# Linear attention fused with a squared-ReLU FFN: k's partition maximum on VectorE, product units split and put at fixed half steps, two tiles moved to the raw buffers

## The chip, the cores and the metric

The kernel runs on one core of one Trainium2 chip. Times are device microseconds of that core. The engines are named as in the profile: PE is TensorE's matmul, PEld its weight load, DVE is VectorE, ACT is ScalarE, POOL is GpSimd, SP is SyncE, whose queue issues nearly all DMAs. "L182" is line 182 of the kernel before. In the span of a profiled execution the time runs from the first to the last instruction.

## The reference

Inputs q, k and v have 8 batches, 8 heads, 576 positions and 64 features. q gets a softmax over its features, k a softmax over its positions. The attention output is q_s (k_s^T v), and it goes through a feed-forward network without biases, 512 to 2048 to 512, with a squared ReLU. Everything is float32.

```python
q_s = exp(q - max(q, axis=-1));  q_s /= sum(q_s, axis=-1) + 1e-9
k_s = exp(k - max(k, axis=2));   k_s /= sum(k_s, axis=2) + 1e-9
kv  = einsum('bhsd,bhse->bhde', k_s, v)
x   = einsum('bhsd,bhde->bhse', q_s, kv)      # -> (4608, 512), heads side by side
out = maximum(x @ w_in, 0)**2 @ w_out
```

The maximum of k is over the 576 positions. A tile of k has positions in its 128 partitions (five to each of the first 64, four to each of the others), so that this maximum is first taken over the positions within a partition and then over the partitions.

## The kernel before

**Feed-forward work.** The 4608 tokens are nine blocks of 512: block b is the first 512 tokens of batch b (in the order of the tiles), and block 8 the 64 left over from each batch. A block has 16 steps, one for each 128 hidden features (fc). Each operand is split into a high and a low float32r part, and a product is three matmuls, hi.hi, hi.lo and lo.hi. So `ffn_h` issues 12 matmuls into an `h_ps` (L317 to L319), `activate` makes r, r*r, `g_hi` and `g_lo` of it on ACT and DVE (L323, L329, L330, L332), and `ffn_out` issues 12 matmuls into four accumulators `o_ps` (L349 to L351). `ffn_out` runs two steps behind `ffn_h` (LAG). In block 0 the weights are loaded and split as well (`split_weight`). At the end of a block `store` takes the four accumulators to four tiles and out (L362 to L376).

**Attention.** The heads of a batch are four pairs, each a list of units from `attention(b, pr)`: `k_max` (maximum of k), `q_exp`, `k_exp` (L189 subtracts the maximum, L190 is the exponential), `q_norm`, `kv` (20 matmuls into `kv_ps`, L228, then kvs), `q_t` (the transposed q) and the products with kv (`at_ps`, L294, emptied by a copy on ACT, L296, and an addition on DVE, L297, into `xf`; x_hi on ACT, L302, and x_lo on POOL, L303). The pairs of batches 0 and 1 (`early`, n < 8) go another way: their maximum over partitions is two small PE operations through PSUM (`m_ps`, `mb_ps`), and their q is transposed on PE (`qt_ps`). From batch 2 on, the "steady" pairs take the maximum with one POOL instruction (L182), transpose q in 32x32 blocks on DVE into `tb` (L214), send `tb` to DRAM (`bounce`, L218) and fetch it in four pieces as `qT` (L221), and split it into `qs` with ACT (L269) and POOL (L270).

**Order.** Batch 0's attention comes first. After that the attention of batch b+1 is emitted in the 16 steps of block b. Each step has two places for units, the two half steps, one behind `ffn_h` and the other behind `ffn_out`; before, the list `todo` of 32 units is spread evenly over what is left of the block's half steps, pair by pair. The order of emission is only a rank: a planner simulates the engines with its own costs and lets a later instruction pass an earlier one that it does not believe ready, so that in the trace an at_ps stands between two matmuls of one h_ps. On the chip each engine then takes its instructions strictly in the planned order. `load_pair`, behind `kv`, loads k, q and v two pairs ahead.

**Buffers.** SBUF tiles with one tag share its buffers in turn. The tag `raw` has three (RAWB): raw weights, `xf`, the stores' `o` and the left-over tokens `xs`. The tags `ke`, `qn`, `q_hi` and `q_lo` have one each; `q_lo` serves `tb` and the second `qs`. The PSUM pool `ps_a` has two buffers for all of `kv_ps`, `at_ps`, `m_ps`, `mb_ps` and `qt_ps`.

## Time and profile before

| | |
|---|---|
| median of 3 runs | 947.51 us (944.28 to 949.34) |
| profiled execution | 947.84 us, its span 946.0 us |
| granted TensorE clock, mean | 0.987 |
| busy: PE, PEld | 893.3, 701.6 us |
| busy: DVE, ACT, POOL | 554.1, 402.3, 200.8 us |
| L182, the maximum on POOL | 24 instructions, 20.5 us busy |
| L214, block transpose of q | 24 instructions, 840 ns each |
| L294, products | 96 matmuls |

Busy time is how long an engine worked on instructions; matmuls overlap one another, so a busy PE need not be at its peak, and the distance between the starts of two matmuls tells more. "Idle before" and the waits tell how long an engine stood and which instruction ended this; the name "issue" means that the engine waited for nothing that the profile shows. Idle time of an engine off the critical path costs nothing by itself.

### The profile page before, as it was taken

Reading aid. Unit: us, or ns where it says so; the run is one execution under the profiler, and the core shown is the slowest. Engines: PE = TensorE matmul, PEld = TensorE weight load, DVE = VectorE, ACT = ScalarE, POOL = GpSimd, SP = SyncE. Lnnn points to the kernel's source line nnn. Section 1 sums busy time; section 2 is a strip of 40 time slices with the busy share of each in tenths; the row PEclk is TensorE's granted clock in tenths of the full one; section 3 lists DMA queues with packets and bytes.
Section 4 is the critical chain, followed back from the end, with each engine's and each line's share of the span. In section 5 each row is a group of like instructions: output and inputs, shape, how many; then the busy total and the mean of one; then the engine's idle time right before and its main releaser. Section 6 shows DMA issues by size and latency. Waiting matters only on the chain.

```text
span 946.0 us, 12435 instructions
## 1 busy us (share of the span) xinstructions
PE 893.3 (94%) x4288; PEld 701.6 (74%) x4288; DVE 554.1 (59%) x1007; ACT 402.3 (43%) x779; POOL 200.8 (21%) x167
## 2 busy tenths in 40 slices
PE   5888889899999999999999999999999999999997
PEld 3566667677787788877887788778877888888885
DVE  7998986666566655557665657566655432223221
ACT  3565663444454444344544445444444422222221
POOL 2444530222222222222222222223122200000000
PEclk9999999999999999999999999999999999999999
DMA  8665552322242223222242214212311020001001
GB/s 199 172 196 176 169 159 70 100 63 78 58 112 67 67 68 93 72 68 68 65 114 68 67 54 119 72 56 67 92 43 37 24 67 1 1 1 45 1 0 45
DMA packets 99454, 73.17 MB, mean 77 GB/s; under 512 B 52288, under 2 KB 89152, under 8 KB 99392
## 3 DMA queue, kind: packets, MB, share of 16 engines
q1 hardware_dynamic: 99232, 72.12, 28.2%
q8 instruction: 34, 0.56, 0.2%
q10 hardware_dynamic: 160, 0.26, 0.1%
q14 instruction: 28, 0.23, 0.1%
HBM read 54.00 MB, written 18.35 MB: 76 GB/s over the span
## 4 chain that ended last, share of the span: by engine, by line
PE 56%; DVE 18%; issue 11%; DMA 8%; SPq 4%; ACT 3%; POOL 1%; DVEq 0%; ACTq 0%
PE o_ps L349 9%; PE o_ps L350 9%; PE o_ps L351 9%; PE h_ps L319 9%; PE h_ps L317 9%; PE h_ps L318 8%; DMA qt<-in_q_dram 3%; SPq L221 2%; DMA raw<-in_moe_w_out_dram 2%; DMA raw<-in_moe_w_in_dram 2%; DVE w L134 2%; PE at_ps L294 2%; DVE ke L189 1%; DVE g_lo L332 1%; DVE xf L297 1%
## 5 line engine op out<-in xcount | busy, mean ns | idle before, releaser
L349 PE MATMUL o_ps<-wo_hi,g_hi 128*128 128x512 f32 x576 | 233.0, 405 | 0.2 <-ACT g_hi L330 0.2
L351 PE MATMUL o_ps<-wo_hi,g_lo 128*128 128x512 f32 x576 | 229.3, 401 | 2.5 <-DVE g_lo L332 2.5
L350 PE MATMUL o_ps<-wo_lo,g_hi 128*128 128x512 f32 x576 | 230.3, 400 | 0.6 <-POOL wo_lo L138 0.6
L317 PE MATMUL h_ps<-x_hi,wi_hi 128*128 128x512 f32 x576 | 227.9, 398 | 1.1 <-ACT x_hi L149 0.7
L319 PE MATMUL h_ps<-x_hi,wi_lo 128*128 128x512 f32 x576 | 228.9, 397 | 0.0
L318 PE MATMUL h_ps<-x_lo,wi_hi 128*128 128x512 f32 x576 | 228.0, 396 | 0.2
L332 DVE TENSOR_TENSOR g_lo<-r,g_hi 128x512 fp32r<-128x512 f32 x141 | 110.4, 783 | 103.9 <-ACT g_hi L330 99.6
L329 DVE TENSOR_TENSOR r<-r 128x512 f32<-128x512 f32 x133 | 99.5, 748 | 117.6 <-ACT r L323 117.5
L323 ACT ACTIVATE r<-h_ps 128x512 f32<-128x512 f32 x144 | 85.5, 595 | 122.2 <-PE h_ps L319 119.6
L351 PEld LDWEIGHTS o_ps<-wo_hi,g_lo 128*128 128x128 f32 x576 | 110.2, 191 | 29.7 <-DVE g_lo L332 4.7
L330 ACT CAST g_hi<-r 128x512 fp32r<-128x512 f32 x144 | 89.2, 621 | 100.5 <-PE o_ps L350 82.9
L350 PEld LDWEIGHTS o_ps<-wo_lo,g_hi 128*128 128x128 f32 x576 | 110.2, 191 | 26.0 <-POOL wo_lo L138 1.0
L349 PEld LDWEIGHTS o_ps<-wo_hi,g_hi 128*128 128x128 f32 x576 | 109.7, 191 | 25.3 <-issue 0.8
L317 PEld LDWEIGHTS h_ps<-x_hi,wi_hi 128*128 128x128 f32 x576 | 108.9, 190 | 26.2 <-ACT x_hi L149 1.1
L318 PEld LDWEIGHTS h_ps<-x_lo,wi_hi 128*128 128x128 f32 x576 | 109.0, 189 | 25.3 <-DVE x_lo L150 0.9
L319 PEld LDWEIGHTS h_ps<-x_hi,wi_lo 128*128 128x128 f32 x576 | 108.9, 189 | 25.4 <-POOL wi_lo L138 0.7
L270 POOL TENSOR_TENSOR qs<-qT,qs 64x640 fp32r<-64x640 f32 x48 | 79.8, 1663 | 95.1 <-ACT qs L269 75.8
L303 POOL TENSOR_TENSOR x_lo<-xf,x_hi 128x256 fp32r<-128x256 f32 x48 | 44.7, 935 | 206.5 <-ACT x_hi L302 71.2
L189 DVE TENSOR_TENSOR ke<-kt,mb 128x640 f32<-128x640 f32 x24 | 19.8, 824 | 84.0 <-POOL mb L182 84.0
L190 ACT ACTIVATE ke<-ke 128x640 f32<-128x640 f32 x32 | 23.6, 738 | 104.4 <-DVE ke L189 104.4
L182 POOL PARTITION_ALL_REDUCE mb<-m x24 | 20.5, 856 | 179.3 <-issue 100.6
L269 ACT CAST qs<-qT 64x640 fp32r<-64x640 f32 x48 | 34.8, 726 | 44.9 <-DMA qT<-bounce 43.9
(82 smaller groups left out, 749.2 us busy)
## 6 DMA issues: line engine op xcount, KB each, us to landing
out_dram<-o SPq DMA_DIRECT2D x70, 128.0 KB, 2.4
raw<-in_moe_w_in_dram SPq DMA_DIRECT2D x16, 512.0 KB, 4.4
raw<-in_moe_w_out_dram SPq DMA_DIRECT2D x16, 512.0 KB, 3.3
bounce<-tb SPq DMA_DIRECT2D x24, 320.0 KB, 2.2
qT<-bounce SPq DMA_DIRECT2D x96, 80.0 KB, 2.2
kt<-in_k_dram SPq DMA_DIRECT2D x32, 160.0 KB, 3.0
qt<-in_q_dram SPq DMA_DIRECT2D x32, 160.0 KB, 3.0
vt<-in_v_dram SPq DMA_DIRECT2D x64, 80.0 KB, 2.6
```

The lines of the kernel that those rows point to most:

```text
L270: nc.gpsimd.tensor_tensor(qs[other], qT[own], qs[own].bitcast(F32), op=ALU.subtract)
L303: nc.gpsimd.tensor_tensor(xl, x[:, :, :HIGH], xh.bitcast(F32), op=ALU.subtract)
L317: nc.tensor.matmul(ps, wi_hi[:, cc, sl], xh[:, cc, :], start=(cc == 0), stop=False)
L318: nc.tensor.matmul(ps, wi_hi[:, cc, sl], xl[:, cc, :], start=False, stop=False)
L319: nc.tensor.matmul(ps, wi_lo[:, cc, sl], xh[:, cc, :], start=False, stop=(cc == NCC - 1))
L323: nc.scalar.activation(r, ps, AF.Relu)
L329: nc.vector.tensor_tensor(r, r, r, op=ALU.mult)
L330: nc.scalar.copy(g_hi, r)
L332: e.tensor_tensor(g_lo, r, g_hi.bitcast(F32), op=ALU.subtract)
L349: nc.tensor.matmul(acc[t], g_hi[:, ts], wo_hi[:, fc, :], start=(n == 0), stop=False)
L350: nc.tensor.matmul(acc[t], g_hi[:, ts], wo_lo[:, fc, :], start=False, stop=False)
L351: prev = nc.tensor.matmul(acc[t], g_lo[:, ts], wo_hi[:, fc, :], start=False, stop=(n == NFC - 1))
```

## The change

1. In steady pairs the maximum over partitions is taken on DVE: `m` (128 partitions by 2 x 64 features) is transposed in 32x32 blocks into `mt`, reduced along the free axis to `m1` (128x4, one partial maximum for each group of 32 partitions and each feature), brought to 32 partitions by four copies (`m4`), reduced over the groups into all four partition groups by four reductions (`m5`), broadcast and transposed back into `mb`. The POOL instruction goes.
2. `k_max` of a steady pair works in a tile of the `raw` tag (`two`), and `ke` is taken only in `k_exp`.
3. `tb` takes a `raw` buffer in place of `q_lo`.
4. `attn` is one product of one head's q and not two: a steady pair has four product units where it had two.
5. `todo` is replaced by `slots`: each unit has a half step of its own. In block 0 pair pr of batch 1 is based at 6 + 6 pr; after that the pairs are 7 half steps apart, from 32 (b - 1) + 1. Offsets follow the order of the units, so a steady pair has k_max at -8, q_exp at -7, q_norm at -5, k_exp at -3, q_t at -1, kv at 0 and the products at 2, 3, 4 and 5. The first pair of batch 2 starts within block 0.
6. `mb` and `left` have one buffer in place of two.

```diff
+FIRST_KV, EARLY_STEP, EARLY_AT = 6, 6, (-6, -5, -3, -2, 0, 1, 2, 3)
+STEADY_STEP, STEADY_AT = 7, (-8, -7, -3, -5, 0, -1, 2, 3, 4, 5)
...
         ps_pool = ps_first if b == 0 and odd else ps_a
 
         def k_max():
-            ke = attn_pool.tile([P, 2, LOW, D], F32, name="ke", tag="q_hi" if odd else "ke", bufs=1)
-            st["ke"] = ke
+            if early:
+                ke = attn_pool.tile([P, 2, LOW, D], F32, name="ke", tag="q_hi" if odd else "ke", bufs=1)
+                st["ke"] = ke
+            else:
+                ke = w_pool.tile([P, 2, 3, D], F32, name="two", tag="raw", bufs=RAWB)
             two, one = ke[:, :, 0:2, :], ke[:, :, 2, :]
             nc.vector.tensor_tensor(two, kk[:, :, 0:2, :], kk[:, :, 2:4, :], op=ALU.max)
             nc.vector.tensor_tensor(one, two[:, :, 0, :], two[:, :, 1, :], op=ALU.max)
...
                 mb = ps_pool.tile([P, 2, 1, D], F32, name="mb_ps", tag="a")
                 nc.tensor.matmul(mb.rearrange("p h o d -> p (h o d)"), mc.broadcast_to([P, P]), ident, start=True, stop=True)
             else:
-                mb = attn_pool.tile([P, 2, 1, D], F32, name="mb")
-                nc.gpsimd.partition_all_reduce(
-                    mb.rearrange("p h o d -> p (h o d)"), m.rearrange("p h d -> p (h d)"), P, bass_isa.ReduceOp.max
-                )
+                mt = attn_pool.tile([P, 4, BLK], F32, name="mt", bufs=1)
+                nc.vector.transpose(mt, m.rearrange("p h (e a) -> p (h e) a", a=BLK))
+                m1 = attn_pool.tile([P, 4], F32, name="m1", bufs=1)
+                nc.vector.tensor_reduce(m1, mt, axis=AX.X, op=ALU.max)
+                m4 = attn_pool.tile([BLK, 4, 4], F32, name="m4", bufs=1)
+                for g in range(4):
+                    nc.vector.tensor_copy(m4[:, g], m1[g * BLK : (g + 1) * BLK])
+                m5 = attn_pool.tile([P, 4, 1], F32, name="m5", bufs=1)
+                for g in range(4):
+                    nc.vector.tensor_reduce(
+                        m5[g * BLK : (g + 1) * BLK, :, 0], m4.rearrange("p g c -> p c g"), axis=AX.X, op=ALU.max
+                    )
+                mb = attn_pool.tile([P, 2, 1, D], F32, name="mb", bufs=1)
+                nc.vector.tensor_copy(mt, m5.broadcast_to([P, 4, BLK]))
+                nc.vector.transpose(mb.rearrange("p h o (e a) -> p (h o e) a", a=BLK), mt)
             st["mb"] = mb
 
         def k_exp():
+            if not early:
+                st["ke"] = attn_pool.tile([P, 2, LOW, D], F32, name="ke", bufs=1)
             ke = st["ke"]
             nc.vector.tensor_tensor(ke, kk, st["mb"].broadcast_to([P, 2, LOW, D]), op=ALU.subtract)
             nc.scalar.activation(ke, ke, AF.Exp)
...
             if early:
                 return
 
-            tb = attn_pool.tile([P, 4, LOW, BLK], F32, name="tb", tag="q_lo", bufs=1)
+            tb = w_pool.tile([P, 4, LOW, BLK], F32, name="tb", tag="raw", bufs=RAWB)
             nc.vector.transpose(
                 tb.rearrange("p c j a -> p j c a"), qn.rearrange("p j h (e a) -> p j (h e) a", a=BLK)
             )
...
                     xh, xl = x_hi[b % 2][:, pr, c0:c1], x_lo[b % 2][:, pr, c0:c1]
                     split(xh, xl, ps)
                 else:
-                    left = attn_pool.tile([P, LEFT], F32, name="left")
+                    left = attn_pool.tile([P, LEFT], F32, name="left", bufs=1)
                     nc.scalar.copy(left, ps)
                     nc.sync.dma_start(x_left[:, pr, b * LEFT : (b + 1) * LEFT], left)
             return go
 
-        def attn(g0, nj):
+        def attn(g0, nj, h):
             def go():
-                N = 2 * nj * BLK
-                xf = w_pool.tile([P, 2, 2, nj, BLK], F32, name="xf", tag="raw", bufs=RAWB)
+                if h == 0:
+                    st[g0] = w_pool.tile([P, 2, 2, nj, BLK], F32, name="xf", tag="raw", bufs=RAWB)
+                xf = st[g0]
                 x, corr = xf[:, 0], xf[:, 1]
-                for h in range(2):
-                    ps = ps_pool.tile([P, 2, nj, BLK], F32, name="at_ps", tag="a")
-                    qs = st["q"][h][:, g0 : g0 + 2, :nj].rearrange("p g j a -> p g (j a)")
-                    nc.tensor.matmul(ps.rearrange("p g j a -> p g (j a)"), kvs[:, h], qs, start=True, stop=True)
-
-                    nc.scalar.copy(corr[half[0]] if h == 0 else corr[half[1]], ps[HALF:])
-                    nc.vector.tensor_tensor(x[half[h]], ps[:HALF], corr[half[h]], op=ALU.add)
+                ps = ps_pool.tile([P, 2, nj, BLK], F32, name="at_ps", tag="a")
+                qs = st["q"][h][:, g0 : g0 + 2, :nj].rearrange("p g j a -> p g (j a)")
+                nc.tensor.matmul(ps.rearrange("p g j a -> p g (j a)"), kvs[:, h], qs, start=True, stop=True)
+
+                nc.scalar.copy(corr[half[h]], ps[HALF:])
+                nc.vector.tensor_tensor(x[half[h]], ps[:HALF], corr[half[h]], op=ALU.add)
+                if h == 0:
+                    return
                 xh, xl = (
                     t[b % 2][:, pr].rearrange("p (j g a) -> p g j a", g=4, a=BLK)[:, g0 : g0 + 2]
                     for t in (x_hi, x_lo)
...
                     nc.sync.dma_start(dst, x[:, :, HIGH])
             return go
 
+        units = [k_max, q_exp, k_exp, q_norm, kv, q_t]
         if early:
-            return [k_max, q_exp, k_exp, q_norm, kv, q_t, attn_early(0, NT), attn_early(NT, S)]
-        return [k_max, q_exp, k_exp, q_norm, kv, q_t, attn(0, LOW), attn(2, HIGH)]
+            return units + [attn_early(0, NT), attn_early(NT, S)]
+        return units + [attn(0, LOW, 0), attn(0, LOW, 1), attn(2, HIGH, 0), attn(2, HIGH, 1)]
 
 
     def h_part(ps, blk, fc, cc):
...
     order0 = list(range(2, PRE)) + list(range(min(2, PRE))) + list(range(PRE, NFC))
     steps = [(0, fc) for fc in order0] + [(blk, fc) for blk in range(1, B + 1) for fc in range(NFC)]
     LAG = 2
-    gs, accs, todo = {}, {}, []
+    gs, accs = {}, {}
+
+    slots = {}
+    for b in range(1, B):
+        for pr in range(NPAIR):
+            if b == 1:
+                base, offs = FIRST_KV + EARLY_STEP * pr, EARLY_AT
+            else:
+                base, offs = 2 * NFC * (b - 1) + 1 + STEADY_STEP * pr, STEADY_AT
+            us = attention(b, pr)
+            nxt = b * NPAIR + pr + NB
+            if nxt < B * NPAIR:
+                us[4] = lambda f=us[4], nxt=nxt: (f(), load_pair(nxt // NPAIR, nxt % NPAIR))
+            for u, o in zip(us, offs):
+                slots.setdefault(base + o, []).append(u)
+    for cc, u in enumerate(left_units()):
+        slots.setdefault(2 * NFC * (B - 1) + 4 + 6 * cc, []).append(u)
     for n in range(len(steps) + LAG):
         if n < len(steps):
             blk, fc = steps[n]
-            if n % NFC == 0:
-                for u in todo:
-                    u()
-                todo = []
-                if blk + 1 < B:
-                    for pr in range(NPAIR):
-                        nxt = (blk + 1) * NPAIR + pr + 2
-                        us = attention(blk + 1, pr)
-                        if nxt < B * NPAIR:
-                            us[4] = lambda f=us[4], nxt=nxt: (f(), load_pair(nxt // NPAIR, nxt % NPAIR))
-                        todo += us
-                elif blk + 1 == B:
-                    todo = left_units()
             if n < PRE:
                 gs[n] = activate(hs[fc], blk, fc)
             else:
...
             for pr in range(NB):
                 load_pair(1, pr)
         m = n - LAG
-        count = -(-len(todo) // max(1, NFC - (2 if blk else 0) - n % NFC)) if n < len(steps) else 0
-        for u in todo[: (count + 1) // 2]:
+        for u in slots.get(2 * n, []):
             u()
-        todo = todo[(count + 1) // 2 :]
         if m >= 0:
             b2, f2 = steps[m]
             if m % NFC == 0:
                 accs[b2] = [ps_o.tile([P, DM], F32, name=f"o_ps{t}", tag="o") for t in range(4)]
             ffn_out(b2, f2, gs.pop(m), accs[b2], m % NFC)
-        for u in todo[: count // 2]:
+        for u in slots.get(2 * n + 1, []):
             u()
-        todo = todo[count // 2 :]
 
 
 # ---- launch: one core; inputs and outputs as the reference has them ----
```

## The prediction, made before the result was known

> **What bounds the kernel now.** I read the page's busy times first, then the span cut at the first output matmul of each token block, then the waits, then two stalls in the timeline.

> ```profile
> span 946.0 us, 12435 instructions
> PE 893.3 (94%) x4288; PEld 701.6 (74%) x4288; DVE 554.1 (59%) x1007; ACT 402.3 (43%) x779; POOL 200.8 (21%) x167
> ```

> TensorE (PE) carries the time; no other engine is busy for two thirds of it. The next view gives, per stretch, its length, then busy time and instructions of PE, weight loads, DVE, ACT and POOL, then the granted clock. The rows are block 0 with the attention of batch 1, blocks 1 to 6 together, each with the attention of the batch after it, block 4 alone as one of these six, and block 7, which has no attention.

> ```profile
> 54.00:174.25 120.25, 109.26 (x505) 83.30 (x506) 105.01 (x173) 69.08 (x128) 41.26 (x27) 0.94 0.52 150
> 174.25:770.42 596.17, 577.19 (x2850) 457.60 (x2849) 356.55 (x659) 265.77 (x531) 140.50 (x118) 0.99 0.26 69
> 475.45:573.65 98.20, 96.22 (x482) 76.35 (x481) 60.78 (x114) 45.32 (x91) 24.04 (x20) 1.00 0.28 74
> 770.42:859.73 89.31, 89.31 (x386) 72.11 (x384) 24.66 (x36) 21.52 (x36) 0.00 (x0) 1.00 0.07 18
> ```

> Block 7 shows the floor: 384 matmuls in 89.31 us with PE never idle, 0.23 us from one start to the next. A block with attention adds 16 product matmuls (at_ps, line 294) and four groups of 20 small ones (kv_ps, line 228). What these must cost is read where nothing waits:

> ```profile
> 537.46 0.39 PE L319 MATMUL h_ps<-x_hi,wi_lo 128*128 128x512 f32 x1
> 537.78 0.80 PE L228 MATMUL kv_ps<-vt,ke 128*64 128x65 f32 x20
> 538.51 0.50 PE L349 MATMUL o_ps<-wo_hi,g_hi 128*128 128x512 f32 x1
> ...
> 545.09 0.39 PE L350 MATMUL o_ps<-wo_lo,g_hi 128*128 128x512 f32 x1
> 545.32 0.46 PE L294 MATMUL at_ps<-qs,kvs 128*128 128x320 f32 x2
> 545.61 0.39 PE L351 MATMUL o_ps<-wo_hi,g_lo 128*128 128x512 f32 x1
> ```

> A kv group adds 538.51 - 537.46 - 0.23 = 0.82 us, two products add 545.61 - 545.09 - 0.23 = 0.29 us. A block with attention therefore needs 89.31 + 4 x 0.82 + 8 x 0.29 = 94.9 us. Six need 569.4, less 0.8 for one kv group that falls outside this stretch: 568.6. They took 596.17. The difference, 27.6 us, is PE waiting, and it is all that a change of the steady attention can win there. The waits name its source:

> ```profile
> ACT ke L190 <- DVE ke L189: 104.4, 27, 7.0
> POOL mb L182 <- issue: 100.6, 17, 6.1
> DVE ke L189 <- POOL mb L182: 84.0, 19, 5.7
> PE at_ps L294 <- DVE xf L297: 13.5, 13, 2.1
> ```

> Before the partition maximum POOL stands 5.9 us (100.6 / 17) waiting for nothing that the trace shows. DVE, which takes its instructions in order, then stands 4.4 us (84.0 / 19) at the subtraction of that maximum, and ACT at the exponential behind it. PE's own longest entry is at_ps, behind the DVE addition (xf) that empties the product's PSUM buffer. One case, engine by engine:

> ```profile
> 514.00 3.21 POOL L270 TENSOR_TENSOR qs<-qT,qs 64x640 fp32r<-64x640 f32 x2 [4.08 <-ACT qs L269]
> 516.47 1.29 DVE L329 TENSOR_TENSOR r<-r 128x512 f32<-128x512 f32 x1
> 518.61 0.28 DVE L171 TENSOR_TENSOR m<-ke,kt 128x128 f32<-128x128 f32 x1
> 523.81 0.82 DVE L189 TENSOR_TENSOR ke<-kt,mb 128x640 f32<-128x640 f32 x1 [4.05 <-POOL mb L182]
> 524.55 0.68 DVE L332 TENSOR_TENSOR g_lo<-r,g_hi 128x512 fp32r<-128x512 f32 x1
> 525.29 0.50 PE L351 MATMUL o_ps<-wo_hi,g_lo 128*128 128x512 f32 x1 [0.16 <-DVE g_lo L332]
> 525.62 0.39 PE L349 MATMUL o_ps<-wo_hi,g_hi 128*128 128x512 f32 x1
> 526.53 0.99 DVE L297 TENSOR_TENSOR xf<-at_ps,xf 64x320 f32<-64x320 f32 x2
> 527.06 0.39 PE L294 MATMUL at_ps<-qs,kvs 128*128 128x256 f32 x1 [1.05 <-DVE xf L297]
> ```

> The maximum m within partitions is ready at 518.9, and its use starts 4.9 us later; g_lo and both xf stand behind it. PE, whose lead is used up by then, waits for g_lo at 525.29 and starts the product at 527.06, 1.44 after the matmul before it instead of 0.23: 1.2 us lost. A second kind of stall has no POOL in it: two product units at each other's heels, four matmuls through two PSUM buffers. Its rows, with the later release of xf by POOL:

> ```profile
> 302.57 0.39 PE L318 MATMUL h_ps<-x_lo,wi_hi 128*128 128x512 f32 x1
> 302.59 0.87 ACT L296 COPY xf<-at_ps 64x320 f32<-64x320 f32 x2
> 303.21 0.99 DVE L297 TENSOR_TENSOR xf<-at_ps,xf 64x320 f32<-64x320 f32 x2
> 303.74 0.39 PE L294 MATMUL at_ps<-qs,kvs 128*128 128x256 f32 x1 [0.78 <-DVE xf L297]
> 307.54 0.74 POOL L303 TENSOR_TENSOR x_lo<-xf,x_hi 128x256 fp32r<-128x256 f32 x1 [7.14 <-ACT xf L296]
> ```

> Here PE loses 303.74 - 302.57 - 0.23 = 0.9 us.

> **The change part by part.** *The all-reduce leaves POOL:* 24 instructions, POOL's stand before them and with it the 84.0 us of DVE. *In its place* DVE gets, per pair, a block transpose of 128x128, a reduction of it to 128x4, four copies and four reductions on 32 partitions each, a broadcasting copy and a second transpose. The nearest rows:

> ```profile
> L214 DVE STREAM_TRANSPOSE tb<-qn 128x640 f32<-128x640 f32 x24 | 20.2, 840 | 3.3 <-PE at_ps L294 2.4 <-PE qt_ps L255 0.9
> L177 DVE TENSOR_REDUCE mc<-m_ps 128x1 f32<-128x128 f32 x8 | 2.2, 274 | 0.3 <-PE m_ps L175 0.3
> L231 DVE RECIPROCAL rs<-rs 128x1 f32<-128x1 f32 x32 | 4.9, 152 | 0.1
> ```

> A 128x128 transpose lies between a fifth of line 214's (0.17 us) and all of it (0.84). I take 0.29, nearer the fifth, since it has a fifth of the elements and even one element takes 0.15. The reduction is line 177's 0.27. The eight small ones lie between 0.07 each, if they overlap as far as half, and 0.27; I take line 231's 0.15. The broadcasting copy lies between 0.15 and the 0.28 of m above, taken as 0.25. Sum: 2 x 0.29 + 0.27 + 8 x 0.15 + 0.25 = 2.3 us, with ends of 1.3 and 4.4; for 24 pairs 55 us, 31 to 106. For a block that is 9.2 us on a DVE busy for 61 of 98, which also loses 84.0 / 6 = 14 us of standing, so it hides under PE's matmuls; were DVE full, it would cost the 9.2. Next in line is ACT's exponential of ke, as now.

> *The four product units* issue the same 16 matmuls, copies, additions and stores per block, but one product per half step (94.9 / 32 = 3.0 us) where a unit had two. A PSUM buffer then has two half steps, 6 us, to be emptied by a copy of 0.4 and an addition of 0.5 (half of the 0.87 and 0.99 above). The planner still reorders, so the half steps are ranks and not times.

> *Raw buffers:* tb no longer waits for the last reader of q_lo (3.3 us in all at line 214, the most that this can win), but two, tb and xf now rotate with the stores through three buffers. At a late buffer DVE would stand with r and g_lo behind it, and PE's line 351 behind those. I take nothing, since the holders are short, and price the loss below. mb goes from two buffers to one, and DVE alone writes and reads it, in order; left too, whose uses in batch 1 lie six half steps apart.

> *Early attention in block 0* now overlaps its pairs and ends four half steps sooner. But mb_ps keeps one of two PSUM buffers for three half steps in which kv_ps, qt_ps and at_ps of the pair before want both, and the first pair of batch 2 adds its k and q chains there. PE idles 120.25 - 109.26 = 11.0 us in this block. A shorter tail may win 6 of them; three waits more, one for each overlapped pair, as long as the longest of at_ps (2.1) may lose 6. I take the middle, nothing.

> *Sum.* Of the 27.6 us I leave 1.5 per block, 9 in all, for starts of kv groups, late kvs or qs and the clock of 0.99. The gain is 18.6. The profiled run took 947.84 us, 1.84 around its span of 946.0; 947.84 - 18.6 = 929.2. The median of the runs, 947.51, is that run's time but for 0.3. I predict 929.

> **The rivals.** *A. Only POOL's part pays.* If the planner bunches products as before, stalls like the 0.9 us at 303.74 stay. One or two a block are 1.4 us; with the 1.5 above, 6 x 2.9 = 17 of 27.6 remain, and the time is 947.8 - 10.2 = 938. For it speaks the planner's freedom, against it the 6 us that a single product has.

> *B. POOL holds up the new chain.* r took 1.29 us at 516.47 (g_lo, of the same shape, 0.68), inside POOL's subtractions from 514.00 to 517.21, and the first maximum of k has a longest of 1730 ns against a median of 415:

> ```profile
> L168 DVE TENSOR_TENSOR ke<-kt x32: 407/415/1730, 4.5 to 713.2; 128x256 f32<-128x256 f32 x32
> ```

> The next pair's k_max now has the half step of q_t, which issues these subtractions. If its operations are held for all 3.2 us, the chain takes 5.5 us. Four of them are 22 us in a block with 37 idle, so DVE does not become the bound; but if at half the pairs xf then comes a microsecond late for PE, 12 us go back, less the fifth or so that spacing absorbs: 939. [...]

> *C. Transposed q comes late: no change.* From q_norm to q_t there are four half steps, 12 us. Transpose, landing of the bounce, four issues and their landing need 0.84 + 2.2 + 1.96 + 2.2 = 7.2. A bounce that stands 10.3 us in SP's queue overshoots by 5.5:

> ```profile
> SPq L101 <- DVE g_lo L332: 81.4, 14, 10.3
> 510.05 1.96 SPq L221 DMA_DIRECT2D qT<-bounce  x4
> bounce<-tb SPq DMA_DIRECT2D x24, 320.0 KB, 2.2
> qT<-bounce SPq DMA_DIRECT2D x96, 80.0 KB, 2.2
> ```

> Three such pairs in the whole run take 16.5 of the 18.6 back: 946. Against it: those queue waits end with DVE work that POOL had held up.

> *D. Slower: the raw ring.* Claims per block rise from 12 (8 xf, 4 stores) to 20. When all three buffers are held by tb and xf, DVE stands for what is left of tb's 3.0 us (0.84 and 2.2), and PE with it. It decides from 1 us of PE per pair, 24 against the gain of 18.6 and the 4.7 below; at the likely 1.3 us the time is 947.8 - 18.6 + 31 = 960. Against it: xf is held for 5.7 us (302.59 to 308.28), so a pair's holds are about 1 + 3.0 + 2 x 5.7 = 15 us, with stores like tb some 74 a block, of 285 that three buffers have.

> **How the numbers follow.** Forecast 0.58, with 917 to 938 as its own range (all of the 27.6 and a little of block 0, or half); A 0.13, B 0.11, C 0.09, D 0.09. About 0.5%, 4.7 us, is what a measurement of this kernel can tell from no change. Faster: 0.58 + 0.13 + 0.11 = 0.82; same 0.09; slower 0.09. The range of 916 to 946 reaches to C and leaves out D and part of C.

> **What would show it.** In the profile after: no line 182 on POOL, no DVE wait for mb, a chain of 2.3 us per pair, blocks 1 to 6 near 96.4 us, PE's wait at at_ps for xf under 4 us. It is wrong if these blocks stay above 98; B shows as stretched maxima and copies, C as at_ps or ACT's qs waiting, D as DVE or ACT standing at a raw buffer. A block 0 that is longer than 120 would show that my nothing there was mis-sized.

## The result and the profile after

The changed kernel takes 916.96 us (median of 4 runs, 915.52 to 917.42) against 946.37 (944.28 to 949.34): a ratio of 0.9684, 95% interval 0.9654 to 0.9715. That is 29.4 us faster; 18.6 had been forecast, as 929 within 916 to 946. The profiled run took 915.52 us with a span of 913.4. The head of its page:

```profile
span 913.4 us, 12612 instructions
PE 879.6 (96%) x4288; PEld 698.0 (76%) x4288; DVE 612.4 (67%) x1295; ACT 400.2 (44%) x779; POOL 178.6 (20%) x143
```

288 instructions were added on DVE and 24 removed on POOL. PE still has its 4288 matmuls. The span, cut again at the first output matmul of each block, in the columns of the prediction (length, then busy time and instructions of PE, weight loads, DVE, ACT and POOL, then the clock): all ahead of block 0's first output matmul, block 0, blocks 1 to 6, block 4 alone.

```profile
0.00:51.90 51.90, 34.88 (x202) 22.06 (x202) 46.77 (x113) 26.70 (x53) 19.11 (x22) 1.00 0.82 203
51.90:167.45 115.55, 105.76 (x496) 79.50 (x497) 110.00 (x191) 66.57 (x125) 39.78 (x28) 0.97 0.52 152
167.45:737.88 570.43, 569.26 (x2860) 459.15 (x2859) 409.20 (x925) 265.63 (x534) 119.73 (x94) 1.00 0.28 73
454.33:549.05 94.72, 94.72 (x483) 76.70 (x481) 71.32 (x162) 44.98 (x90) 20.60 (x16) 1.00 0.29 78
```

Blocks 1 to 6 fell from 596.17 to 570.43, 1.8 above the floor of 568.6 that the prediction had worked out; block 4 runs without a gap on PE. The other 6.8 us of the span's 32.6 were won ahead of block 1: block 0 from 120.25 to 115.55, and 54.0 to 51.9 ahead of it. The marks do not cut off the same work, though: ten matmuls of block 1's h_ps ran in block 0 before and run behind the mark now (2850 recorded in blocks 1 to 6 before, 2860 here). At 0.23 us each that is 2.3 us, so that like for like blocks 1 to 6 won 28.0 and block 0 2.4. DVE no longer waits for mb. The waits after that answer to those shown of before:

```profile
POOL x_lo L326 <- ACT x_hi L325: 355.5, 34, 21.9
ACT ke L211 <- DVE rs L252: 28.4, 13, 5.1
ACT ke L211 <- DVE ke L210: 23.4, 10, 4.7
ACT xf L317 <- DMA out_dram<-o: 11.1, 4, 3.6
PE at_ps L315 <- ACT kvs L267: 1.0, 1, 1.0
```

POOL now simply waits for work. ACT's idle time before the exponential of ke went from 104.4 us to 52.4; only 23.4 of these are now put down to DVE's ke. PE's largest entry for the at_ps of steady pairs (L315) is a single one of 1.0 us, and none names xf. The new DVE instructions, by line (count, then busy time and mean in ns):

```profile
L190 DVE STREAM_TRANSPOSE mt<-m 128x128 f32<-128x128 f32 x24 | 7.3, 305 | 0.4
L192 DVE TENSOR_REDUCE m<-mt 128x4 f32<-128x128 f32 x24 | 6.7, 280 | 0.5
L195 DVE COPY m<-m 32x4 f32<-32x4 f32 x96 | 16.4, 171 | 1.6
L198 DVE TENSOR_REDUCE m<-m 32x4 f32<-32x16 f32 x96 | 16.3, 170 | 1.6
L202 DVE COPY mt<-m 128x128 f32<-128x128 f32 x24 | 9.9, 413 | 0.4
L203 DVE STREAM_TRANSPOSE mb<-mt 128x128 f32<-128x128 f32 x24 | 7.4, 309 | 0.5
```

m1, m4 and m5 all appear as "m". A chain has 305 + 280 + 4 x 171 + 4 x 170 + 413 + 309 = 2671 ns of DVE time, against the 2.3 us put down for it.

### The profile page after: what moved, and what is told of

It reads as the page before. It is cut to its first block, busy times and chain, and to the rows that moved or that the text cites. A ratio compares the mean times of both kernels' runs of the same rounds, so it can differ in the third digit from the quotient of the medians.

```text
span 913.4 us, 12612 instructions
## 1 busy us (share of the span) xinstructions
PE 879.6 (96%) x4288; PEld 698.0 (76%) x4288; DVE 612.4 (67%) x1295; ACT 400.2 (44%) x779; POOL 178.6 (20%) x143
## 4 chain that ended last, share of the span: by engine, by line
PE 80%; DVE 12%; DMA 3%; issue 2%; SPq 1%; ACT 1%; POOL 0%; DVEq 0%; ACTq 0%
PE o_ps L373 13%; PE o_ps L374 13%; PE o_ps L375 13%; PE h_ps L341 13%; PE h_ps L343 13%; PE h_ps L342 12%; DMA raw<-in_moe_w_in_dram 2%; DVE w L137 2%; DVE raw L136 2%; PE kv_ps L249 2%; PE at_ps L315 1%; DVE raw L135 1%; DVE g_lo L356 1%; DMA raw<-in_moe_w_out_dram 1%; DVE ke L210 1%
## 5 line engine op out<-in xcount | busy, mean ns | idle before, releaser
L373 PE MATMUL o_ps<-wo_hi,g_hi 128*128 128x512 f32 x576 | 227.7, 400 | 1.7 <-ACT wo_hi L139 1.1
L353 DVE TENSOR_TENSOR r<-r 128x512 f32<-128x512 f32 x133 | 97.2, 731 | 114.3 <-ACT r L347 113.3
L326 POOL TENSOR_TENSOR x_lo<-xf,x_hi 128x256 fp32r<-128x256 f32 x48 | 42.1, 877 | 356.6 <-ACT x_hi L325 355.5
L291 POOL TENSOR_TENSOR qs<-qT,qs 64x640 fp32r<-64x640 f32 x48 | 81.1, 1689 | 109.2 <-ACT qs L290 97.8
L317 ACT COPY xf<-at_ps 64x320 f32<-64x320 f32 (+1 forms) x96 | 38.0, 396 | 31.1 <-PE at_ps L315 16.2
L318 DVE TENSOR_TENSOR xf<-at_ps,xf 64x320 f32<-64x320 f32 (+1 forms) x96 | 42.5, 443 | 8.5 <-ACT xf L317 6.9
L211 ACT ACTIVATE ke<-ke 128x640 f32<-128x640 f32 x32 | 23.6, 739 | 52.4 <-DVE rs L252 28.4
```

The source lines that it names most:

```text
L291: nc.gpsimd.tensor_tensor(qs[other], qT[own], qs[own].bitcast(F32), op=ALU.subtract)
L318: nc.vector.tensor_tensor(x[half[h]], ps[:HALF], corr[half[h]], op=ALU.add)
L353: nc.vector.tensor_tensor(r, r, r, op=ALU.mult)
L373: nc.tensor.matmul(acc[t], g_hi[:, ts], wo_hi[:, fc, :], start=(n == 0), stop=False)
```

## The experiments

Each ran in several rounds beside the kernel before. "Blocks 1 to 6" is the stretch from block 1's first output matmul to block 7's; as the planner takes more or fewer of block 1's h_ps matmuls ahead of the first of these marks, the matmuls recorded in the stretch (0.23 us each) and the start of block 7 stand beside it. The tail from there is 175.5 to 175.9 us in every kernel.

| kernel | median us | ratio to before, 95% | blocks 1 to 6 | matmuls in it | block 7 starts at |
|---|---|---|---|---|---|
| before | 946 to 949 | | 596.2 | 2850 | 770.4 |
| changed | 916.96 | 0.965 to 0.972 | 570.4 | 2860 | 737.9 |
| e1: before, maximum on DVE | 916.90 | 0.964 to 0.970 | 566.5 | 2851 | 739.7 |
| e2: changed, maximum on POOL | 996.34 | 1.046 to 1.056 | 654.5 | 2862 | 823.5 |
| e3: changed, two products a unit | 918.65 | 0.966 to 0.972 | 572.5 | 2861 | 741.0 |
| e4: changed, early units as before | 920.54 | 0.968 to 0.974 | 565.9 | 2849 | 742.5 |
| e5: before, POOL runs maxima only | 917.27 | 0.967 to 0.972 | 565.8 | 2850 | 739.2 |
| e6: changed, k_max two half steps later | 914.88 | 0.964 to 0.969 | 569.8 | 2862 | 737.4 |
| e7: changed, chain twice | 947.94 | 0.996 to 1.002 | 597.7 | 2863 | 767.5 |
| e8: changed, two raw buffers | 922.53 | 0.972 to 0.979 | 567.4 | 2836 | 745.5 |
| e9: e7 with k_max as in e6 | 943.58 | 0.994 to 0.997 | 600.5 | 2862 | 768.8 |
| e10: e6, block 0 relieved on DVE | 917.84 | 0.965 to 0.971 | 570.6 | 2861 | 741.4 |
| e11: e1 with the chain twice | 935.10 | 0.984 to 0.989 | 585.1 | 2851 | 757.5 |
| e12: e7, qs's low half on DVE | 922.19 | 0.970 to 0.976 | 577.2 | 2862 | 745.4 |

**e1: the maximum alone.** The `else` branch of `k_max` in the kernel before is replaced by the new chain; units, places, `tb` and `ke` stay as they were.

```diff
-                mb = attn_pool.tile([P, 2, 1, D], F32, name="mb")
-                nc.gpsimd.partition_all_reduce(
-                    mb.rearrange("p h o d -> p (h o d)"), m.rearrange("p h d -> p (h d)"), P, bass_isa.ReduceOp.max
-                )
+                mt = attn_pool.tile([P, 4, BLK], F32, name="mt", bufs=1)
+                nc.vector.transpose(mt, m.rearrange("p h (e a) -> p (h e) a", a=BLK))
...
+                nc.vector.transpose(mb.rearrange("p h o (e a) -> p (h o e) a", a=BLK), mt)
...
-                    left = attn_pool.tile([P, LEFT], F32, name="left")
+                    left = attn_pool.tile([P, LEFT], F32, name="left", bufs=1)
```

> The kernel before with the partition maximum on DVE and nothing else of the change (mb and left with one buffer each, which the new small tiles need for their room). Stretch of blocks 1 to 6: 596.2 us before, 570.4 after the whole change, floor 568.6. Theory (POOL's stand makes the larger part of PE's waiting, two products in one unit the rest, about 1.4 us a block): 578 to 582 and a total of 929 to 933. Rival 1 (spacing alone, because a product with 6 us can wait out POOL's stand): over 590, total over 941. Rival 2 (POOL's stand is all): 572, total 919 to 924.

```profile
173.18:739.71 566.53, 566.32 (x2851) 457.66 (x2849) 413.10 (x938) 267.33 (x532) 116.42 (x95) 1.00 0.28 73
```

916.90 us: the whole gain, with two products in a unit, units dealt out from the list and `tb` in q_lo. In 566.53 us of blocks 1 to 6 PE is not busy for 0.2. The theory of two sources of waiting falls, and rival 2, that POOL's stand is all of it, holds, with a little more than it had promised. The stall at 303.74 that the prediction took for a second kind has POOL's stand just ahead of it in the kernel before:

```profile
299.68 0.72 POOL L182 PARTITION_ALL_REDUCE mb<-m  x1 [5.88 <-issue]
300.43 0.83 DVE L189 TENSOR_TENSOR ke<-kt,mb 128x640 f32<-128x640 f32 x1 [5.50 <-POOL mb L182]
```

DVE came out of 5.50 us of standing at 300.43. ACT's part of r had ended at 294.53, yet DVE took r only behind that ke, at 301.18; r, g_lo and the additions that PE waited for had queued there and followed until 304.20. So the bunched products had cost PE time because DVE, behind POOL's stand, came late to empty them.

**e2: the converse.** All of the change but the maximum, which is POOL's again.

```diff
-                mt = attn_pool.tile([P, 4, BLK], F32, name="mt", bufs=1)
...
+                mb = attn_pool.tile([P, 2, 1, D], F32, name="mb")
+                nc.gpsimd.partition_all_reduce(
+                    mb.rearrange("p h o d -> p (h o d)"), m.rearrange("p h d -> p (h d)"), P, bass_isa.ReduceOp.max
+                )
```

> The changed kernel with the maximum given back to POOL's all-reduce in steady pairs; split products, half steps and raw buffers stay. Theory: DVE again stands some 4 us per pair, single products outlast most of it, g_lo does not: 2 us a block come back, blocks 1 to 6 at 580 to 585, total 927 to 932. Rival 1 (spacing alone): 572, total 917 to 919. Rival 2 (POOL's stand is all): over 590, total over 937.

996.34 us: rival 2 had said over 937, but not this much; with the maximum on POOL the new order is slower than the old one by 5%. Blocks 1 to 6, the waits, then POOL's timeline around an all-reduce, with ACT's casts of qs:

```profile
168.93:823.47 654.54, 598.68 (x2862) 477.33 (x2860) 352.64 (x657) 262.78 (x530) 133.11 (x116) 0.95 0.24 62
POOL x_lo L315 <- issue: 84.7, 12, 7.5
POOL qs L280 <- issue: 28.6, 4, 7.5
PE at_ps L304 <- POOL qs L280: 22.9, 6, 4.6
PE h_ps L331 <- POOL x_lo L315: 16.8, 5, 4.2
```

```profile
472.06 0.73 POOL L315 TENSOR_TENSOR x_lo<-xf,x_hi 128x256 fp32r<-128x256 f32 x1 [7.30 <-issue]
478.04 1.48 ACT L279 CAST qs<-qT 64x640 fp32r<-64x640 f32 x2 [1.42 <-DMA qT<-bounce]
478.78 0.72 POOL L190 PARTITION_ALL_REDUCE mb<-m  x1 [5.99 <-ACT qs L279]
487.04 0.71 POOL L315 TENSOR_TENSOR x_lo<-xf,x_hi 128x256 fp32r<-128x256 f32 x1 [7.53 <-issue]
487.83 3.16 POOL L280 TENSOR_TENSOR qs<-qT,qs 64x640 fp32r<-64x640 f32 x2
```

POOL stands not only before the all-reduce but also 7.1 us (84.7 / 12) before the x_lo that follows one, and the same before qs. Here the all-reduce at 478.78 comes ahead of an x_lo and of the subtractions for qs, so both stands delay what PE needs next: ACT's casts of qs ended at 479.5, and POOL began to subtract at 487.83. PE's granted clock fell too, to 0.95 from 0.99 in these blocks; 0.05 of 654.5 us is some 33 us, an estimate, so the waits are not the whole price. In the kernel before, too, x_lo had 42.9 us of such stands in 6 places, but nobody waited for it soon.

**e3: two products a unit**, in the changed kernel.

```diff
-STEADY_STEP, STEADY_AT = 7, (-8, -7, -3, -5, 0, -1, 2, 3, 4, 5)
+STEADY_STEP, STEADY_AT = 7, (-8, -7, -3, -5, 0, -1, 2, 4)
...
-        return units + [attn(0, LOW, 0), attn(0, LOW, 1), attn(2, HIGH, 0), attn(2, HIGH, 1)]
+        return units + [lambda: (attn(0, LOW, 0)(), attn(0, LOW, 1)()), lambda: (attn(2, HIGH, 0)(), attn(2, HIGH, 1)())]
```

> The changed kernel with two products in a unit again, the units at half steps 2 and 4 behind kv. Theory: one or two stalls of 0.9 us per block come back, blocks 1 to 6 at 576 to 580, total 922 to 927. Rival 1 (spacing is what counts): over 585, total over 931. Rival 2 (POOL's stand is all): 570 to 572, total 917.

918.65 us, 1.7 above the changed kernel but from another set of runs, blocks 1 to 6 at 572.5: the split is worth about 2 us at most. This and e1 agree.

**e4: early units as before**, in the changed kernel.

```diff
-FIRST_KV, EARLY_STEP, EARLY_AT = 6, 6, (-6, -5, -3, -2, 0, 1, 2, 3)
+FIRST_KV, EARLY_STEP, EARLY_AT = 4, 8, (-4, -3, -2, -1, 0, 1, 2, 3)
```

> The changed kernel with batch 1's units in block 0 at the half steps that they had before (8 per pair, one after the other, up to the last half step). The change won 2.1 us ahead of block 0's first output matmul and 4.7 us in block 0 (120.3 to 115.6). Theory that the overlap of early pairs won this: block 0 goes back to 119 to 121 and the total to 921 to 924. Rival (it came from elsewhere, the freed q_lo, POOL or the planner's order): block 0 stays within 1 us of 115.6, total 916 to 918.

```profile
53.66:176.59 122.93, 110.50 (x506) 84.80 (x507) 110.64 (x198) 69.28 (x129) 40.27 (x27) 0.93 0.52 152
```

920.54 us, 3.6 above the changed kernel. The two come from different sets of runs and the intervals of their ratios overlap, but block 7 starts 4.6 us later in the trace, so the overlapped early pairs seem to win some 4 us within the new order. Block 0 takes 122.9, with ten matmuls more ahead of the mark (x506 for x496), and its clock is 0.93 where the changed kernel has 0.97. The clock alone could make 5.1 us (0.07 x 122.9 - 0.03 x 115.6, an estimate); whether the early pairs won by fewer waits or by the clock is not shown. But e1 has the old early order and reaches block 7 2.8 us before e4, so the early places are not where the change as a whole won; they make up for what the rest of the new order costs there.

**e5: what POOL's stand is.** The kernel before, its maximum on POOL; the two other steady jobs of POOL go to DVE.

```diff
-                    nc.gpsimd.tensor_tensor(qs[other], qT[own], qs[own].bitcast(F32), op=ALU.subtract)
+                    nc.vector.tensor_tensor(qs[other], qT[own], qs[own].bitcast(F32), op=ALU.subtract)
...
-                nc.gpsimd.tensor_tensor(xl, x[:, :, :HIGH], xh.bitcast(F32), op=ALU.subtract)
+                nc.vector.tensor_tensor(xl, x[:, :, :HIGH], xh.bitcast(F32), op=ALU.subtract)
```

> The kernel before, its maximum still on POOL, with POOL's two other steady jobs (the low half of qs, L270, and x_lo, L303) on DVE, so that from batch 2 on POOL runs all-reduces and nothing else. Theory after the first four runs: POOL's stand of 5.9 us before an all-reduce, and of 7.3 us before the next x_lo, is a change of POOL's program from one kind of instruction to the other, not a price of the all-reduce. Then the stand before mb goes almost wholly, blocks 1 to 6 take 566 to 573 us (596.2 before), total 916 to 923, although DVE gets some 10 us a block more. Rival (every all-reduce pays its 5.9 us): DVE goes on standing 4 us per pair, blocks 1 to 6 at 588 to 600, total 938 to 950.

First the instructions of the maximum in the kernel before, where the second row counts the entries named MODIFY_POOL_CONFIG in POOL's queue at that line, then the same rows here:

```profile
L182 POOL PARTITION_ALL_REDUCE mb<-m x24: 722/722/3330, 138.5 to 720.7; - x24
L182 POOLq MODIFY_POOL_CONFIG  x46: 1/6/21, 125.3 to 714.8; - x46
```

```profile
L182 POOL PARTITION_ALL_REDUCE mb<-m x24: 702/734/3330, 136.9 to 684.4; - x24
L182 POOLq MODIFY_POOL_CONFIG  x2: 8/8/8, 125.3 to 125.3; - x2
...
POOL mb L182 <- DVE m L171: 401.3, 19, 28.5
DVE ke L189 <- POOL mb L182: 0.9, 2, 0.6
```

917.27 us with the maximum still on POOL. Of the 46 entries two are left, both at 125.3, POOL's waits before the maximum are all put down to DVE and none to "issue", an all-reduce takes 0.73 us (median), and DVE's stand has gone from 84.0 us to 0.9. So the stand was not the price of a partition maximum but of POOL going back and forth between two kinds of instruction, some 6 us one way (5.9 in the kernel before) and 7 the other (7.1 in e2). What POOL does in that time no trace shows.

**e6: k_max two half steps later**, in the changed kernel.

```diff
-STEADY_STEP, STEADY_AT = 7, (-8, -7, -3, -5, 0, -1, 2, 3, 4, 5)
+STEADY_STEP, STEADY_AT = 7, (-6, -7, -3, -5, 0, -1, 2, 3, 4, 5)
```

> The changed kernel with a steady pair's k_max two half steps later (offset -6 for -8), so that it no longer has the half step of the pair before's q_t and its POOL subtractions. In the changed kernel the first, second and third maximum have longest times of 1508, 1644 and 1668 ns, the small copies 728, the broadcasting copy 1400. Theory (POOL's subtractions hold these up, and PE does not notice): the mean of the three maxima and of the broadcasting copy falls by a third or more, total stays within 2 us of 917. Rival (holding up the chain costs PE time): total falls by 2 us or more. Other rival (k_max two half steps later makes k_exp late): total over 920.

In the changed kernel, durations by line (least, median and longest ns):

```profile
L175 DVE TENSOR_TENSOR two<-two x24: 223/274/1644, 127.7 to 672.0; 128x128 f32<-128x128 f32 x24
L195 DVE COPY m<-m x96: 150/158/728, 137.5 to 677.4; 32x4 f32<-32x4 f32 x96
L198 DVE TENSOR_REDUCE m<-m x96: 156/171/177, 141.5 to 678.1; 32x4 f32<-32x16 f32 x96
L202 DVE COPY mt<-m x24: 183/226/1400, 144.8 to 678.4; 128x128 f32<-128x128 f32 x24
```

The broadcasting copy fell from a mean of 413 to 280 ns, but the third maximum stayed at 688 (691 in the changed kernel) and the second went from 497 to 453, as if the planner pulled these forward whatever their rank. The expected third was not reached, and the run does not tell apart what it was for. 914.88 us (914.55 to 915.55) is the lowest time of all, 2.1 us under the changed kernel, but from another set of runs, and the intervals of the two ratios overlap.

**e7: the chain twice**, to see what hides it.

```diff
+                for _ in range(2):
+                    nc.vector.transpose(mt, m.rearrange("p h (e a) -> p (h e) a", a=BLK))
...
+                    nc.vector.transpose(mb.rearrange("p h o (e a) -> p (h o e) a", a=BLK), mt)
```

> The changed kernel with DVE's twelve new instructions of each steady pair run twice, with the same result. One pass takes 305 + 280 + 4 x 171 + 4 x 170 + 413 + 309 = 2671 ns of DVE time, so a block has 10.7 us more on a DVE that is busy for 71 of 94.7. Theory (the chain lies under PE's matmuls): blocks 1 to 6 stay at 570 to 573, total 916 to 919. Rival (DVE is close to being the bound, or the chain is on the way of the products): 10 to 60 us more, total 927 to 977.

947.94 us: 27 us more in blocks 1 to 6, and the gain is gone. Blocks 1 to 6, PE's largest entry for at_ps (L316 here), the groups of the second and third maximum, then POOL and DVE around one kv and the product that PE wanted:

```profile
169.81:767.52 597.71, 577.63 (x2863) 462.31 (x2861) 471.49 (x1205) 265.27 (x536) 124.47 (x94) 0.99 0.27 70
PE at_ps L316 <- DVE kvs L153: 15.8, 7, 3.6
L175 DVE TENSOR_TENSOR two<-two 128x128 f32<-128x128 f32 x24 | 12.7, 527 | 0.0
L177 DVE TENSOR_TENSOR m<-two,kt 128x128 f32<-128x128 f32 x24 | 20.5, 854 | 0.4
```

```profile
502.22 3.75 POOL L292 TENSOR_TENSOR qs<-qT,qs 64x640 fp32r<-64x640 f32 x2 [2.75 <-ACT qs L291]
502.56 1.36 DVE L175 TENSOR_TENSOR two<-two 128x128 f32<-128x128 f32 x1
504.45 1.67 DVE L177 TENSOR_TENSOR m<-two,kt 128x128 f32<-128x128 f32 x1
514.61 0.46 DVE L153 TENSOR_TENSOR kvs<-kf,kvs 64x64 fp32r<-64x64 f32 x2
514.96 0.39 PE L316 MATMUL at_ps<-qs,kvs 128*128 128x320 f32 x1 [3.35 <-DVE kvs L153]
```

DVE is busy for 79% of these blocks (471.5 of 597.7 us), yet from 496.3 to 515.1 us no gap on it exceeds 0.05 us: x's additions, the next pair's q and k work, the chain and kvs fall together around this kv. The planned order of PE has the product earlier than that: PE stands 3.35 us at it, and so in seven places, 15.8 us in all.

**e8: two raw buffers**, in the changed kernel.

```diff
-RAWB = 3
+RAWB = 2
```

> The changed kernel with two raw buffers for three. It prices rival D of the prediction, which had holds of some 74 us a block: of 190 buffer microseconds that is two fifths. Theory (the ring has slack in blocks 1 to 6, but weights in block 0 need it): blocks 1 to 6 within 4 us of 570.4, block 0 and the start longer by 3 to 10, total 922 to 931. Rival (the ring is tight, and three buffers just suffice): blocks 1 to 6 longer by 15 us or more, total over 935.

```profile
54.10:178.05 123.95, 113.54 (x520) 83.56 (x521) 111.98 (x197) 69.35 (x130) 40.58 (x28) 0.97 0.50 148
178.05:745.48 567.43, 565.04 (x2836) 454.43 (x2835) 424.08 (x918) 262.80 (x530) 121.27 (x94) 1.00 0.27 72
```

922.53 us. Here 24 matmuls more than in the changed kernel lie ahead of block 1's mark (x520 for x496 in block 0), some 5.5 us. Like for like, blocks 1 to 6 lose 2.5 us with two buffers (567.43 + 5.5 - 570.43), block 0, where weights pass through the ring, 2.9, and the start 2.2. Rival D of the prediction, which had put 31 us on the ring with three buffers, falls.

**e9: e7 with k_max at -6.** The diff is that of e6 on top of e7.

> The chain run twice, as in the run with 947.94 us, and k_max at offset -6 in place of -8, so that it stands behind kv of the pair before in the ranks and no longer just ahead of it. Twice the chain cost 27 us in blocks 1 to 6 (597.7 against 570.4) with DVE busy for 82 of 99 us a block, and PE's waits were at_ps for kvs. Theory (place, not amount: the chain stood between kv_ps and kvs on DVE, and the products had been planned too early for it): with the same DVE work blocks 1 to 6 come down to 570 to 580, total 915 to 925. Rival (amount: DVE at 82 of 95 us has too little left): blocks 1 to 6 at 590 or more, total over 935.

943.58 us and 600.5 in blocks 1 to 6. The theory that the rank of k_max decides falls, as e6 would suggest. The rival's result came, but not its reason, as e12 shows.

**e10: block 0 relieved**, on top of e6.

```diff
-SQUARES_ACT = 11
+SQUARES_ACT = 16
...
-W_LOW_POOL = 26
+W_LOW_POOL = 32
```

> The kernel with k_max at offset -6 (914.88 us), and in block 0 all squares on ACT (16 for 11) and the low parts of all 32 weight chunks on POOL (32 for 26). That takes 5 x 0.68 + 6 x 0.69 = 7.5 us off DVE, which is busy for about 110 of 115 us there. Theory (what is left beside the floor is DVE in block 0): block 0 shorter by 2 to 7, total 908 to 913. Rival (PE's idle there is waits in chains, not DVE's time): within 2 us, total 913 to 917; longer if POOL's 1.4 us a chunk comes late.

917.84 us, and block 0 takes 117.3 us where e6 has 114.6 (at a clock of 0.96 for 0.97). DVE is still busy for 108.1 of them although 7.5 us had been taken off; which work of other blocks filled this in is not shown. The theory falls for block 0; what holds up the rest there stays open.

**e11: the chain twice in e1.** The loop of e7 around the chain of e1.

> The kernel before with the maximum on DVE alone (916.9 us) and that chain run twice. Theory (the new places give no slack that the old order lacks, since both have the maximum's chain ahead of late kvs): blocks 1 to 6 lose as much as in the new order, 20 to 35 us, total 937 to 952. Rival (the old order holds k_max behind kv of the pair before, because its units follow each other): blocks 1 to 6 within 8 us of the 566.5 with one chain, total 917 to 925, and the new order is then the one that is more easily upset.

935.10 us: 18.5 us more than e1 in blocks 1 to 6. The old order is upset as well, less than the new one. Neither theory's number was met; the old order has somewhat more slack around kv, where PE waits for kvs 6.6 us in all (15.8 in e7).

**e12: the chain twice, without POOL beside it.**

```diff
-                    nc.gpsimd.tensor_tensor(qs[other], qT[own], qs[own].bitcast(F32), op=ALU.subtract)
+                    nc.vector.tensor_tensor(qs[other], qT[own], qs[own].bitcast(F32), op=ALU.subtract)
```

> The changed kernel with the chain twice (947.94 us) and the low half of qs (L291) taken from POOL to DVE, so that POOL's 3.2 to 3.7 us of subtractions no longer stand beside the next pair's maxima and copies. In the run with the chain twice DVE works without a gap from 496.3 to 515.1 us, and kvs comes 3.4 us late for at_ps; POOL holds up the second and third maximum and a copy there by (1.36 - 0.27) + (1.67 - 0.28) + (1.17 - 0.68) = 3.0 us, and the two subtractions on DVE take some 2 x 0.8 = 1.6. Theory (the burst of DVE work around kv decides, with POOL's holds in it): the burst is 1.4 us shorter, blocks 1 to 6 go from 597.7 to 580 to 592, total 930 to 942. Rival (DVE's amount of work decides; it is 6 us a block more): blocks 1 to 6 at 600 or more, total 950 to 985.

```profile
168.21:745.41 577.20, 572.33 (x2862) 458.34 (x2861) 470.15 (x1255) 264.36 (x536) 41.14 (x48) 1.00 0.28 73
PE at_ps L316 <- DVE kvs L153: 2.4, 2, 1.4
L292 DVE TENSOR_TENSOR qs<-qT,qs 64x640 fp32r<-64x640 f32 x48 | 39.4, 821 | 4.2 <-ACT qs L291 3.0
L175 DVE TENSOR_TENSOR two<-two 128x128 f32<-128x128 f32 x24 | 7.1, 295 | 0.1
L177 DVE TENSOR_TENSOR m<-two,kt 128x128 f32<-128x128 f32 x24 | 7.0, 291 | 0.6
```

922.19 us: 25.8 less than e7, with 39.4 us of work moved onto DVE. The second maximum falls from 527 to 295 ns and the third from 854 to 291, and DVE is busy for 470.2 us of blocks 1 to 6 as against 471.5, for its other work takes about as much less as was added. PE's waits for kvs fall from 15.8 us to 2.4. Since e7 had no wait of PE for qs, it is not an earlier qs that helped. Part of the gain may be clock, which is 0.99 in these blocks in e7 and 1.00 in e12: some 6 us (0.01 x 597.7, an estimate). Blocks 3 to 6 are back at 93.7 to 95.3; blocks 1 and 2 still take 99. So in e7 it was the work and POOL's holds together, at the one place where DVE has no room, and not the amount of DVE's work. The 577.2 us of blocks 1 to 6 lie just below the 580 to 592 that the theory had expected; the rival's 600 is excluded.

## Why the prediction was right, and where it was not

**The number.** 916.96 lies inside the range of 916 to 946 by 1 us, and just below the 917 at which the forecast's own range began: 29.4 us were won for 18.6 forecast, and the terms that were off (the 9 us left over, ten matmuls missing from the 596.17, and nothing for block 0 and the start) erred the same way. That the range held it was in part luck.

**PE's floor** (94.9 us a block) held: block 4 takes 94.72, and e5 runs 2850 matmuls of blocks 1 to 6 in 565.8 us, where the 568.6 less ten matmuls is 566.3. But the prediction set the 596.17 of before, without ten of the six blocks' matmuls, against the floor with them. Like for like 29.9 us were to be won and not 27.6, and 28.0 were. Nor is all of it PE standing, as the prediction says: PE's idle time there fell from 19.0 us (596.17 - 577.19) to 1.2, and the rest is in its busy time, of which up to 3.4 us is the clock (an estimate from two stretches of 3.4 us at half clock before, from 232.3 and 327.9, and none after). What makes up the remainder stays open.

**The all-reduce leaves POOL:** right, and more than had been said. It is the whole of what was won (e1); what the prediction called a second kind of stall with no POOL in it, at 303.74, was the first kind's consequence, 3 us behind a stand of DVE for POOL.

**The mis-sized term is the 9 us left over.** Block by block, 1.5 us had been kept for kv's starts, late kvs or qs and the clock. Measured are 1.8 us for all six (570.43 - 568.6, with all their matmuls), and the clock there rose from 0.99 to 1.00. With 1.8 for 9 the forecast would have been 922.

**The chain's cost:** 2.3 us per pair were put down, 2.67 came, with medians that sum to 2.44 (306 + 285 + 4 x 158 + 4 x 171 + 226 + 311); the rest are the longest copies, up to 1400 ns. That it hides was right, but the reason given, 37 idle us of DVE a block, was not: e7 adds another 10.7 us a block and loses 27 us in all. Idle time averaged over a block does not say what is free where the work falls.

**The four products** had been given the role of a second source of gain. They have next to none (e3: 1.7 us; e1: none). Rival A, which rested on the same idea, is gone with it.

**Raw buffers** at nothing: right for PE (e8), though the ring is felt: ACT stands 11.1 us at xf behind stores (1.4 in the kernel before). **Block 0** at nothing: 4.7 us were won there, 2.4 like for like, inside the 6 either way that the prediction kept, and 2.1 ahead of it, for which it had no term. In e4, some 4 us go with the overlapped early pairs, within the new order. The clock of block 0 rose from 0.94 to 0.97, which alone could make 3.7 us (0.06 x 120.25 - 0.03 x 115.55, an estimate); what won it is not settled.

**The rivals.** B's hold-up is there and its price was not: the second maximum's longest time is 1644 ns, the broadcasting copy's 1400, and no reduction of L198 exceeds 177 ns. That copies would stretch was the author's estimate, since the rows in the prediction have long times of r (1.29 us) and of a maximum (1730 ns) alone. In the changed kernel all 30 maxima and copies of k_max that took over 1.3 times the median of their line ran beside an instruction of POOL, while 38 reductions of L198 did so and none is long. PE pays nothing measurable for it at one chain; at two, taking POOL's subtractions for qs away gives back 20.5 of 27.3 us (e7, e12). C: no wait of PE for qs after the change. D: its sign is there in ACT's 11.1 us, but PE waits for no xf (and e8).

## What to carry to other kernels

When an engine stands before one instruction and the profile names nobody, look at what it ran before and after: if it changes from one kind of instruction to another, give it one kind only (e5), or take the odd one off (e1); either brought the whole gain here, and doing half of a redesign around it made things worse (e2). POOL's stall showed up as several kinds of wait elsewhere (in the kernel before as DVE's 84.0 us for mb and ACT's 104.4 for ke behind it, 0.9 and 21.1 in e5, and as PE's 13.5 for xf); undo one part at a time before crediting any of them. Judge cover by the stretch in which the new work falls, with what another engine holds up there, and not by an engine's idle share.

## What the runs showed of the hardware beyond that

PE's granted clock fell to 0.50 after some of its waits. In the kernel before, first the product behind a wait, then two stretches of 3.4 us:

```profile
231.51 0.39 PE L294 MATMUL at_ps<-qs,kvs 128*128 128x256 f32 x1 [2.08 <-DVE xf L297]
232.30:235.70 3.40, 3.40 (x10) 2.62 (x10) 2.71 (x5) 1.96 (x5) 0.22 (x1) 0.50 0.07 12
235.70:239.10 3.40, 3.40 (x16) 2.78 (x15) 3.06 (x7) 1.83 (x4) 1.74 (x2) 1.00 0.45 149
```

From 0.8 us after this wait of 2.08 us the granted clock is 0.50 for 3.4 us, with 10 matmuls where the next 3.4 us have 16. The kernel before has six such stretches of 3.4 us and the changed kernel two (those at the very end left out). Each begins within 5 us of idle times of PE that come to 1.7 us or more; not every such idle time is followed by one (2.01 us up to 179.45 in the kernel before was not: the next stretch begins at 232.30). That the waits cause it is inferred from this order in time.
